# Which way pairs 14 and 15 are turned: TensorE, or DRAM and transposing DMAs

## The chip, the cores and the metric

The kernel runs on one core of a Trainium2 chip. The metric is the device time of one execution in microseconds (us). The core has a matrix engine (TensorE, in profiles PE, its weight loads PEld), three engines for elementwise work (VectorE or DVE, ScalarE or ACT, GpSimd or POOL), and SyncE (SP), whose queue issues most of this kernel's transfers. The core's 16 DMA engines move the data between DRAM and the on-chip memory (SBUF). Matmuls write their results into the 8 banks of a second memory, PSUM.

## The reference

Causal attention with 16 extra "beacon" keys in front, followed by a feed-forward net of three maxed branches:

```python
B, H, S, D, Nb = 8, 8, 576, 64, 16
k_all = concatenate([beacon_k, k], axis=2)        # beacons are seen by every query
v_all = concatenate([beacon_v, v], axis=2)
scores = matmul(q, k_all.T) / sqrt(D)             # later keys masked out
a = exp(scores - max) ; a /= a.sum(-1)
attn = matmul(a, v_all)                           # (B, H, S, D)
x = attn.transpose(0, 2, 1, 3).reshape(B * S, H * D)       # 4608 x 512
h = maximum(maximum(x @ w1, x @ w2), x @ w3)      # 512 -> 768
out = h @ w_out                                   # 768 -> 512
```

Inputs and output are float32.

## The kernel before

The 64 heads (8 batches of 8) are worked off as 32 **pairs** of heads, four pairs to a batch; pair p belongs to batch p // 4. Two pairs make a quad. One pass of the main loop is a **step** and belongs to one pair.

To multiply q and k, TensorE needs them with the head's 64 dimensions on the partitions, that is, transposed. Four buffers `qTs` and four `kTs` hold transposed pairs, pair p in buffer p % 4. There are two ways in which a pair gets there, and both start alike: `load_pair` (L225) brings q and k as float32 into a staging tile `st` (a rotation of 8 tiles, which V's pieces share), and `cast_pair` (L260, on GpSimd) makes bfloat16 tiles of them (rotations of 4 each).

- **On TensorE**, pairs 0 to 15: `turn_pair(p)` makes 12 transposes of 96 x 128 (six for q, six for k, L387) into two PSUM banks. VectorE copies k out of PSUM (L433), ScalarE or VectorE copies q (L422), and `place_beacons` (L429) copies the 16 beacon columns of k from `bT`, where they lie ready.
- **Through DRAM**, pairs 16 to 31: `store_pair` (L372) writes the bfloat16 tiles to a scratch tile in DRAM, and `fetch_pair` (L379 and L380) reads them back with DMAs that transpose. `open_dram` (L363) makes the scratch tiles of a batch and writes its beacons ahead of k, so that they come along with the fetch.

In the main loop, from pair 8 on, a step p emits this:

1. `emit_burst(p)`: 12 score matmuls (L495) into all 8 PSUM banks, with ScalarE's exponentials (L513) behind them into `at_sb`.
2. At even p, `emit_pv_whole`: the 72 matmuls of values and sums (L615) of the two pairs before.
3. GpSimd's causal masks (L535) on this pair's `at_sb`.
4. Units of the feed-forward net (L691 for the first layer, L739 for the second), as many as a schedule allows. Output tiles y go out on SP's queue (L771). After the first unit stands `turn_pair(p + 1)`, if pair p + 1 is turned on TensorE; after the second unit, the work that `plan` holds for (p, 0). What it holds for (p, 1) comes at the end of the step.

`plan` is filled by hand, by step. For a pair p turned on TensorE the cast stands in step p - 2. For a pair through DRAM the cast stands in step p - 5, the store in step p - 4 and the fetch in step p - 3. Each cast is followed by `next_load`, which issues the next load of the list `loads`; that list is sorted by the step in which the loaded data is cast, and within a step by a second number (0 for pairs turned on TensorE, 1 for pieces of V, 2 for pairs through DRAM). With the load of pair 16 go the loads of the beacon keys of batches 4 to 7, which are cast together in step 11 (`bk16`). Those of batches 1 to 3 were cast long before (`bk16_1`).

All loads, stores, fetches and outputs stand in SP's one queue, in the order in which they are emitted. An instruction that waits there holds all that are behind it.

Of the kernel before, what the change touches and what calls it, by code (L numbers as in the profile page):

```python
# [17 lines left out]
def kernel(  # L18
# [15 lines left out]
    B, H, S, D = q.shape  # L34
    Nb = beacon_k.shape[2]
# [25 lines left out]
    PPB = H // 2  # L61
    PPQ = PPB // n_quad
    NPAIR = B * PPB
    RING = 4

    B_PE = 4

# [46 lines left out]
    ffn_h = ctx.enter_context(tc.tile_pool(name="ffn_h", bufs=2))  # L116
    ffn_y = ctx.enter_context(tc.tile_pool(name="ffn_y", bufs=5))
    psum = ctx.enter_context(tc.tile_pool(name="psum", bufs=1, space=PSUM))
    dram_pool = ctx.enter_context(tc.tile_pool(name="dram", bufs=B - B_PE, space=bass.MemoryType.DRAM))

    N_BANK = 8
    acc = psum.tile([128, N_BANK, 512], FP32, name="acc")
# [48 lines left out]
    xT = const.tile([128, n_ct, RING * S], BF16, name="xT")  # L171
    NB_PE = Nb * B_PE
    NB_DMA = Nb * (B - B_PE)
    bT = const.tile([128, PPB, NB_PE], BF16, name="bT")
# [3 lines left out]
    bk16_1 = const.tile([NB_PE - Nb, H, D], BF16, name="bk16_1")  # L178
    bk32 = const.tile([NB_DMA, H, D], FP32, name="bk32")
    bk16 = const.tile([NB_DMA, H, D], BF16, name="bk16")  # L180
# [153 lines left out]
    def load_beacons(b0, b1, dst, queue=None):  # L334
        for b in range(b0, b1):
            (queue or nc.sync).dma_start(
                out=dst[Nb * (b - b0) : Nb * (b - b0 + 1)],
                in_=beacon_k[b].rearrange("h n d -> n h d"),
            )
# [19 lines left out]
    def open_dram(b):  # L359
        q_dram[b] = dram_pool.tile([PPB, S, 2 * D], BF16, name="q_dram")  # L360
        k_dram[b] = dram_pool.tile([PPB, NK, 2 * D], BF16, name="k_dram")
        lo = Nb * (b - B_PE)
        nc.sync.dma_start(  # L363
            out=k_dram[b][:, 0:Nb].rearrange("i n x -> n i x"),
            in_=bk16[lo : lo + Nb].rearrange("n (i h) d -> n i (h d)", h=2),
        )

    def store_pair(p):
# [135 lines left out]
    def emit_burst(p):  # L504
        at[p] = at_pool.tile([128, AT_W], BF16, name="at_sb")
        for gi, first in enumerate(next_pairs()):
            off = 0
            for t, q0, q1 in groups(p)[gi]:
                for e in range(2):
                    score(p, t, e, q0, q1, acc[:, first + e, off : off + q1 - q0])  # L510
                off += q1 - q0
            for e0, e1 in ((0, 1), (1, 2)) if gi == 0 else ((0, 2),):
                nc.scalar.activation(  # L513
                    out=both_heads(p, gi)[:, e0:e1],
                    in_=acc[:, first + e0 : first + e1, 0 : g_width(p, gi)],
                    func=AF.Exp,
                    scale=scale,
                )
# [250 lines left out]
    def store_y(n):  # L769
        for c0, y in y_out[:n]:  # L770
            nc.sync.dma_start(out[c0 : c0 + 128, :], y)  # L771
        del y_out[:n]
# [20 lines left out]
    def may_emit(limit, ahead=0):  # L793
        n = done[0] + ahead
        return n < END and n + 1 <= limit + 1e-6 and units[n][0] <= ready[0]
# [13 lines left out]
    def at_step(p, g, *fns):  # L809
        plan.setdefault((p, g), []).extend(fns)  # L810

    def L(fn, *a):
        return lambda: fn(*a)

    def cast_step(p):
        return (p - 2, 0) if p < B_PE * PPB else (p - 5, int(p < 19))

    def v_step(b, piece):
        return (b * PPB + 1, piece)

    def load_turned_pair(p, **gate):
        if p == B_PE * PPB:
            load_beacons(B_PE, B, bk32)
        load_pair(p, **gate)

    loads = [(cast_step(p), 2 * (p >= B_PE * PPB), partial(load_turned_pair, p)) for p in range(2 * PPB, NPAIR)]
    loads += [(v_step(b, i), 1, partial(load_v, b, i)) for b in range(2, B) for i in range(2)]
    loads = [load for _, _, load in sorted(loads, key=lambda x: x[:2])]

# [5 lines left out]
    def C(fn, *a):  # L835
        def run():
            fn(*a)
            next_load()

        return run  # L840

    def start():
        keep_busy(8, 480)
        load_half(0, 0, nc.sync)
        load_half(0, 1, nc.scalar)
        load_half(1, 0, nc.sync)
        load_beacons(0, 1, bk32_0, nc.scalar)
        load_half(1, 1, nc.scalar)
        make_identity(nc, ident)
        nc.gpsimd.memset(tri, 1.0)  # L850
        nc.gpsimd.affine_select(
            out=tri,
            in_=tri,
            compare_op=ALU.is_ge,
            fill=0.0,
            base=0,
            pattern=[[1, 128]],
            channel_multiplier=-1,
        )
        load_quad(1, 0)  # L860
        load_quad(0, 1)
        load_quad(1, 1)
        load_v(0, 0)
        load_v(0, 1)
        load_beacons(1, B_PE, bk32_1)
        cast_half(0, 0, by_dve)
        cast_half(0, 1, by_act)
        by_dve(bk16_0, bk32_0)
        turn_part(0, 0, 0, 6, by_act)
        turn_part(0, 0, 1, 7)  # L870
        keep_busy(3)
        turn_beacons(0, 1, bk16_0)
        cast_half(1, 0, by_dve)
        cast_half(1, 1, by_dve)
        keep_busy(2)
        turn_part(1, 0, 0, 4)
        turn_part(1, 0, 1, 5)
# [94 lines left out]
    def second_batch():  # L972
        for p in range(PPB, 2 * PPB):
            place_beacons(p + 1, by_act)
            emit_burst(p)
            for gi in range(NG):
                emit_masks(p, gi)
                if p < PPB + 2 and 0 < gi < 3:
                    cast_piece(p + 2, gi - 1, by_pool)
                if p == 2 * PPB - 1 and gi == 1:  # L980
                    cast_v(1, 1, by_pool)
                    next_load(gate=nc.gpsimd)
                    next_load(3)
            if p < PPB + 2:
                stage.pop(("pair", p + 2))
            if p == PPB + 2:
                load_w_out()
                cast_v(1, 0, by_pool)
            if p + 1 < 2 * PPB:
                turn_pair(p + 1, by_dve)  # L990
                F(2, next_psum)
        F(4, next_psum)
        for p in range(2 * PPB, 2 * PPB + 2):
            cast_pair(p, by_pool, by_pool)
            next_load()
        finish = emit_pv_whole(n_quad)
        turn_pair(2 * PPB, by_dve)
        F(2, next_psum)
        finish()

    for p in range(B_PE * PPB, NPAIR):
        if p % PPB == 0:
            at_step(p - 4, 0, L(open_dram, p // PPB))
        at_step(p - 3, 0, L(fetch_pair, p))
        at_step(p - 4, 0, L(store_pair, p))
    for p in range(2 * PPB + 2, B_PE * PPB):
        at_step(*cast_step(p), C(cast_pair, p, by_pool, by_pool))
    for b in range(2, B):
        for i in range(2):
            at_step(*v_step(b, i), C(cast_v, b, i, by_pool))  # L1010
    at_step(B_PE * PPB - 5, 1, L(by_pool, bk16, bk32))
    for p in range(B_PE * PPB, NPAIR):
        at_step(*cast_step(p), C(cast_pair, p, by_pool, by_pool))


    def emit_all():
        start()
        first_batch()
        second_batch()
        n_y = 0  # L1020
        v_tiles.pop(0)

        for p in range(2 * PPB, NPAIR):
            b, pi = divmod(p, PPB)
            emit_burst(p)
            finish = emit_pv_whole(p // 2 - 1) if p % 2 == 0 else None
            for gi in range(NG):
                emit_masks(p, gi)
            allowed = (b - 1) * UPB + (-2, 4, 10, 16)[pi]
            n = 0  # L1030
            while may_emit(allowed):
                n_y = len(y_out)
                close = not may_emit(allowed, 1)
                emit_ffn(allowed, last_pair() if close else next_psum, close)
                store_y(n_y)
                n += 1
                if n == 1 and p + 1 < B_PE * PPB:
                    turn_pair(p + 1, by_act)
                    place_beacons(p + 1, by_act)
                if n == 2:  # L1040
                    for fn in plan.pop((p, 0), ()):
                        fn()
            assert n >= 2
            if finish:
                finish()
            for s in range(2):
                for fn in plan.pop((p, s), ()):
                    fn()
            if pi == 0:
                v_tiles.pop(b - 1)  # L1050
        assert not plan and not loads
        finish = emit_pv_whole(NPAIR // 2 - 1)
        for _ in range(4):
            emit_ffn(END, next_psum)
        finish()
        store_y(len(y_out))
        while emit_ffn(END - 1, next_psum):
            store_y(len(y_out))
        mm2_last(n_tokb - 1, TOKB // 128 - 1, (0, 320, 512))
# [33 lines left out]
```

## Time and profile before

| | |
|---|---|
| median of 3 runs | 286.55 us (285.75 to 287.72) |
| the profiled execution | 285.18 us, span 283.5 us |
| granted TensorE clock | 1.00 |
| TensorE | 97% busy; 144 transposes at L387 |
| VectorE, ScalarE, GpSimd | 61%, 56%, 48% busy |
| stores `q_dram<-p`, `k_dram<-p` | 16 each, 144 KB, median 2.3 us to landing |
| fetches `qT<-q_dram`, `kT<-k_dram` | 16 each, median 4.3 and 3.5 us to landing |
| loads of q and k per pair | 28 each, 288 KB, median 5.3 and 5.5 us to landing |

The span runs from the first to the last instruction of the profiled execution; 1.7 us of its time lie around it. The profile is of a single execution, 1.37 us below the median of the timed runs. "To landing" counts from the start of the issuing instruction on its queue to the moment when the data is there, and so has in it the time that a transfer stands behind others.

### The profile page before, as it was taken

To read this page: it belongs to the slowest core of one execution; us is meant where nothing else is said; L and a number is where in the kernel's file an instruction comes from. 1 tells how busy PE (TensorE), PEld (TensorE's weight loads), DVE (VectorE), ACT (ScalarE), POOL (GpSimd) and SP (SyncE) were. 2 spreads that over 40 slices of the span, in tenths; PEclk is the share of its full clock that TensorE was granted. 3 is DMA by queue.
4 is the path that set the end of the run, shared out by engine and by line. 5 is a ranking of instruction groups with operands and counts; after the bars stand their busy time and mean duration, and the time that the engine had idled before them with its cause. 6 is when DMAs were issued, how large, how long until landed. Compare 5 with 4: busy or idle time off the path is not lost.

```text
span 283.5 us, 7622 instructions
## 1 busy us (share of the span) xinstructions
PE 274.7 (97%) x2996; PEld 156.4 (55%) x2996; DVE 172.7 (61%) x303; ACT 159.4 (56%) x299; POOL 136.4 (48%) x282
## 2 busy tenths in 40 slices
PE   7889999999999999999999999999999999999995
PEld 3466664555555555555556787555555554444442
DVE  3774765583856658274836383638363847876873
ACT  3697595896668576858585858585767640000000
POOL 7263789287376865466556746583346210000000
PEclk9999999999999999999999999999999999999999
DMA  7999999999999999999999999999451003004004
GB/s 146 193 198 222 246 225 178 240 201 295 276 226 235 255 265 203 226 222 240 250 213 225 267 254 183 216 258 218 121 156 39 0 2 146 2 1 150 0 0 148
DMA packets 85315, 50.59 MB, mean 178 GB/s; under 512 B 64416, under 2 KB 80032, under 8 KB 85280
## 3 DMA queue, kind: packets, MB, share of 16 engines
q1 hardware_dynamic: 80672, 45.76, 71.8%
q0 software_dynamic: 4048, 4.03, 9.0%
q8 instruction: 23, 0.38, 0.6%
q10 hardware_dynamic: 560, 0.33, 0.5%
q14 instruction: 12, 0.10, 0.1%
HBM read 35.13 MB, written 14.22 MB: 174 GB/s over the span
## 4 chain that ended last, share of the span: by engine, by line
PE 82%; DVE 1%; issue 0%
PE acc L691 46%; PE acc L739 16%; PE acc L615 11%; PE acc L495 7%; PE acc L387 2%; PE acc L757 0%; DVE hT L709 0%; DVE qT L422 0%; DVE y L764 0%; DVE kT L433 0%
## 5 line engine op out<-in xcount | busy, mean ns | idle before, releaser
L691 PE MATMUL acc<-xT,w_sb 128*128 128x512 bf16 (+4 forms) x744 | 135.3, 338 | 0.0
L709 DVE TENSOR_TENSOR hT<-hT,acc 128x512 bf16<-128x512 bf16 x102 | 70.0, 687 | 59.2 <-PE acc L691 50.0
L691 PEld LDWEIGHTS <-w_sb 128*128 128x128 bf16 x744 | 69.2, 98 | 59.7
L535 POOL TENSOR_SCALAR_AFFINE_SELECT at_sb<-at_sb 128x256 bf16<-128x256 bf16 (+2 forms) x176 | 62.8, 378 | 71.1 <-ACT at_sb L513 69.4
L513 ACT ACTIVATE at_sb<-acc 128x208 bf16<-128x208 f32 (+3 forms) x140 | 89.5, 737 | 5.9 <-PE acc L495 4.6
L260 POOL CAST p<-st 96x768 bf16<-96x768 f32 x56 | 44.7, 821 | 9.3 <-PE acc L615 5.1
L739 PE MATMUL acc<-w_out_sb,hT 128*128 128x512 bf16 (+2 forms) x246 | 48.4, 348 | 0.0
L711 ACT CAST hT<-acc 128x352 bf16<-128x352 f32 x18 | 8.1, 452 | 47.0 <-PE acc L691 47.0
L739 PEld LDWEIGHTS <-hT 128*128 128x128 bf16 x246 | 22.6, 98 | 21.7 <-DVE hT L709 1.6
L746 DVE COPY y<-acc 128x512 f32<-128x512 f32 (+1 forms) x35 | 21.9, 628 | 20.5 <-PE acc L739 14.8
L711 DVE CAST hT<-acc 128x512 bf16<-128x512 f32 (+1 forms) x48 | 26.6, 554 | 9.4 <-PE acc L691 9.1
L495 PE MATMUL acc<-qT,kT 64*128 64x208 bf16 (+1 forms) x336 | 26.9, 280 | 1.1 <-DVE hT L730 0.6
L764 ACT COPY y<-acc 128x320 f32<-128x320 f32 x1 | 0.4, 426 | 46.0 <-PE acc L757 46.0
L495 PEld LDWEIGHTS <-kT 64*128 64x128 bf16 x336 | 15.5, 94 | 13.3 <-issue 2.6
L615 PE MATMUL acc<-at_sb,v_sb 128*32 128x512 bf16 (+5 forms) x672 | 22.8, 281 | 0.0
L638 DVE TENSOR_TENSOR xT<-raw,recip 128x576 bf16<-128x576 f32 x28 | 21.8, 821 | 0.0
L625 ACT COPY raw<-acc 128x512 f32<-128x512 f32 x28 | 15.8, 637 | 4.5 <-PE acc L615 4.3
L305 POOL CAST v_sb<-st 128x1536 bf16<-128x1536 f32 (+2 forms) x21 | 18.3, 893 | 0.0
L615 PEld LDWEIGHTS <-v_sb 128*32 128x32 bf16 (+1 forms) x672 | 14.5, 96 | 6.7
L489 ACT ACTIVATE at_sb<-acc 128x1024 bf16<-128x1024 f32 (+3 forms) x16 | 13.1, 860 | 3.6 <-PE acc L480 3.5
L615 PE MATMUL acc<-at_sb,ones 128*32 128x512 bf16 (+3 forms) x336 | 14.9, 284 | 0.0
L433 DVE COPY kT<-acc 128x576 bf16<-128x576 bf16 x12 | 9.0, 752 | 6.3 <-PE acc L387 6.3
(69 smaller groups left out, 170.5 us busy)
## 6 DMA issues: line engine op xcount, KB each, us to landing
out_dram<-y SPq DMA_DIRECT2D x35, 256.0 KB, 3.5
st<-in_q_dram SPq DMA_DIRECT2D x28, 288.0 KB, 5.3
st<-in_k_dram SPq DMA_DIRECT2D x28, 288.0 KB, 5.5
st<-in_v_dram SPq DMA_DIRECT2D x24, 256.0 KB, 6.7
w_sb<-in_moe_w_dram POOLq DMA_DIRECT2D x6, 384.0 KB, 7.7
q_dram<-p SPq DMA_DIRECT2D x16, 144.0 KB, 2.3
k_dram<-p SPq DMA_DIRECT2D x16, 144.0 KB, 2.3
st<-in_v_dram SPq DMA_DIRECT2D x8, 224.0 KB, 6.4
```

Source lines behind the costliest of these rows:

```text
L260: cast(t16.rearrange("p r h d -> p h r d"), st[0:QP, i * NQ2 : (i + 1) * NQ2].rearrange("p (h r d) -> p h r d", h=2, r=QR),)
L305: cast(v_sb[0:n, t:t1].rearrange("p t h d -> p (t h d)"), st[0:n, (t - t_lo) * H * D : (t1 - t_lo) * H * D],)
L495: nc.tensor.matmul(ps, kTs[p % NT][hs, 128 * t : 128 * t + 128], qTs[p % NT][hs, q0:q1], start=True, stop=True, tile_position=(64 * e, 0),)
L513: nc.scalar.activation(out=both_heads(p, gi)[:, e0:e1], in_=acc[:, first + e0 : first + e1, 0 : g_width(p, gi)], func=AF.Exp, scale=scale,)
L535: nc.gpsimd.affine_select(out=view, in_=view, compare_op=ALU.is_ge, fill=0.0, base=x0, pattern=[[0, 2], [1, hi - lo]], channel_multiplier=-1,)
L615: nc.tensor.matmul(acc[32 * j : 32 * j + 32, bank, lo + q0 - qa : lo + qb - qa], lhsT, at_view(PPQ * quad + j // 2, t, j % 2, q0, qb), sta ...
L638: nc.vector.tensor_mul(xT[:, 2 * g + i, c0 : c0 + S], raw[:, i], recip)
L691: nc.tensor.matmul(ps[:, a:b], w_in[i][:, ct, 128 * ft : 128 * (ft + 1)], xT[:, ct, x0 : x0 + b - a], start=(ct == 0), stop=(ct == n_ct - 1),)
L709: nc.vector.tensor_max(h[:, lo:hi], h[:, lo:hi], ps[:, lo:hi])
L711: (by_act if hi < TOKB else by_dve)(h[:, lo:hi], ps[:, lo:hi])
L739: nc.tensor.matmul(ps[:, lo:hi], hT[:, ft, 128 * tt : 128 * (tt + 1)], w_out_sb[:, ft, lo:hi], start=(ft == 0), stop=(ft == n_ft - 1),)
L746: (by_act if hi < d_model else by_dve)(y[:, lo:hi], ps[:, lo:hi])
```

## The change

A number `FIRST_DMA = 14` takes the place of `B_PE * PPB = 16` where the kernel decides which pairs go through DRAM. Pairs 14 and 15, the last two of batch 3, are cast in steps 10 and 11 (instead of 12 and 13), stored in steps 11 and 12 and fetched in steps 12 and 13, all three one step later against their burst than for pairs 16 and up. Batch 3 gets scratch tiles in DRAM, of which these two pairs use the second half; its beacons are written there, for all four pairs, from `bk16_1`. The loads of pairs 14 and 15 get the second number 2, and their place in the list of loads follows the new cast steps. `turn_pair` and `place_beacons` are no longer called for these two.

```diff
+    FIRST_DMA = 14
...
-    dram_pool = ctx.enter_context(tc.tile_pool(name="dram", bufs=B - B_PE, space=bass.MemoryType.DRAM))
+    dram_pool = ctx.enter_context(tc.tile_pool(name="dram", bufs=B - FIRST_DMA // PPB, space=bass.MemoryType.DRAM))
...
     def open_dram(b):
...
-        lo = Nb * (b - B_PE)
+        src, lo = (bk16, Nb * (b - B_PE)) if b >= B_PE else (bk16_1, Nb * (b - 1))
...
-            in_=bk16[lo : lo + Nb].rearrange("n (i h) d -> n i (h d)", h=2),
+            in_=src[lo : lo + Nb].rearrange("n (i h) d -> n i (h d)", h=2),
...
     def cast_step(p):
-        return (p - 2, 0) if p < B_PE * PPB else (p - 5, int(p < 19))
+        if p < FIRST_DMA:
+            return (p - 2, 0)
+        return (p - 4, 0) if p < B_PE * PPB else (p - 5, int(p < 19))
+
+    def store_step(p):
+        return p - 3 if p < B_PE * PPB else p - 4
...
-    loads = [(cast_step(p), 2 * (p >= B_PE * PPB), partial(load_turned_pair, p)) for p in range(2 * PPB, NPAIR)]
+    loads = [(cast_step(p), 2 * (p >= FIRST_DMA), partial(load_turned_pair, p)) for p in range(2 * PPB, NPAIR)]
...
-    for p in range(B_PE * PPB, NPAIR):
-        if p % PPB == 0:
-            at_step(p - 4, 0, L(open_dram, p // PPB))
-        at_step(p - 3, 0, L(fetch_pair, p))
-        at_step(p - 4, 0, L(store_pair, p))
-    for p in range(2 * PPB + 2, B_PE * PPB):
+    for p in range(FIRST_DMA, NPAIR):
+        if p == FIRST_DMA or p % PPB == 0:
+            at_step(store_step(p), 0, L(open_dram, p // PPB))
+        at_step(store_step(p) + 1, 0, L(fetch_pair, p))
+        at_step(store_step(p), 0, L(store_pair, p))
+    for p in range(2 * PPB + 2, FIRST_DMA):
         at_step(*cast_step(p), C(cast_pair, p, by_pool, by_pool))
...
-    for p in range(B_PE * PPB, NPAIR):
+    for p in range(FIRST_DMA, NPAIR):
         at_step(*cast_step(p), C(cast_pair, p, by_pool, by_pool))
...
-                if n == 1 and p + 1 < B_PE * PPB:
+                if n == 1 and p + 1 < FIRST_DMA:
                     turn_pair(p + 1, by_act)
                     place_beacons(p + 1, by_act)
```

## The prediction

> **What bounds the kernel now.** I read the page's first two parts, then the chain of waits in order of time, then SP's timeline, and last single transfers (issue and landing). The page first: the engines' busy time, and the busy tenths in 40 slices.
>
> ```profile
> PE 274.7 (97%) x2996; PEld 156.4 (55%) x2996; DVE 172.7 (61%) x303; ACT 159.4 (56%) x299; POOL 136.4 (48%) x282
> ...
> PE   7889999999999999999999999999999999999995
> ...
> DMA  7999999999999999999999999999451003004004
> ```
>
> TensorE is full from the fourth slice on, at a granted clock of 1.00. But the DMA engines are full too, up to about 200 us, and the change takes work from the first and gives it to the second. So two things are to be read: how much of TensorE's time the removed transposes are, and how far ahead of TensorE the transfers run. The chain that ended last, stage by stage (start, length, engine and line):
>
> ```profile
> 90.34 0.84 PE acc L495 x12
> 91.18 1.40 PE acc L739 x6
> 92.58 0.51 PE acc L387 x12
> 93.09 1.30 PE acc L739 x6
> 94.39 3.46 PE acc L691 x20
> 97.85 0.85 PE acc L495 x10
> 98.70 2.25 PE acc L615 x71
> 100.95 0.97 PE acc L691 x4
> 101.92 0.51 PE acc L387 x12
> 102.43 4.33 PE acc L691 x24
> 106.76 0.85 PE acc L495 x11
> ...
> 120.45 0.83 PE acc L495 x12
> 121.28 2.70 PE acc L739 x12
> 123.98 3.46 PE acc L691 x20
> 127.44 0.85 PE acc L495 x11
> 128.29 2.25 PE acc L615 x72
> 130.54 5.29 PE acc L691 x28
> ```
>
> L495 opens the step of each pair: 13 at 90.34, 14 at 97.85, 15 at 106.76, 17 at 120.45, 18 at 127.44, 19 at 135.84 (the next line of that view). From 53 us to the end every piece is TensorE's and each starts where the last ends, so no other engine and no transfer holds it up, and what is taken out of it there comes off the end. L387 is the turning: pair 14 at 92.58 in step 13, pair 15 at 101.92 in step 14.
>
> **What is removed.** 24 transposes, 12 for each pair. In the chain 12 cost 0.51 us, 43 ns each. A second way gives the same: step 17 has the matmuls of step 13 without a turn, and step 18 those of step 14. 7.51 - 6.99 = 0.52 and 8.91 - 8.40 = 0.51. So **1.03 us leave the path**. The same comparison says what happens without the two PSUM banks of a turn: steps 17 and 18 run so and show no gap, so I add nothing for banks. Two copies on VectorE (L433, mean 752 ns) and four on ScalarE (L422, 648, and L429, 228) go as well, 1.5 and 1.75 us; neither engine is on the path (61% and 56% busy), so this gains nothing. The groups' table gives a transpose a mean of 206 ns, which would make 24 of them 4.9 us; but 12 start within 0.51 us, so they overlap, and the chain's 43 ns is the price.
>
> [...]
>
> **What is added, on the queue of SP.** Four transposing transfers (L379, L380, issue 1.14 and 1.23 us), four stores (L372, 0.38 to 0.52), one of beacons (L363, 0.57 to 1.30): about 4.8 + 1.8 + 0.9 = 7.5 us, in steps 11 to 13. SP's own waits say what can cover this: between 75.6 and 113 us it stood 1.2 + 0.8 + 2.4 + 1.2 + 1.5 + 0.8 = 7.9 us for other engines. SP's order there now:
>
> ```profile
> 77.56 7.98 SPq L289 DMA_DIRECT2D st<-in_v_dram  x5
> 85.66 1.30 SPq L363 DMA_DIRECT2D k_dram<-bk  x1
> ...
> 93.85 1.24 SPq L379 DMA_TRANSPOSE qT<-q_dram  x1
> 95.15 1.24 SPq L380 DMA_TRANSPOSE kT<-k_dram  x1
> ```
>
> The third of the five V pieces is issued at 79.05 and holds the queue for 4.09 us: here SP goes as fast as transfers land. The first fetch now is pair 16's, issued at 93.85 and landed 3.3 and 2.6 us after each issue, at 97.7, for a burst that starts at 112.9: 15 us early. Pair 14 has less: its fetch stands one step later against its burst (two steps ahead, not three), and its burst starts at 97.85 - 0.52 = **97.3**.
>
> When does it land? Transfers of the queue land one behind the other. Up to that V piece the same loads go out as now, in another order, so it still lands at 79.05 + 8.1 = 87.1. Behind it come, by the gaps between landings now: beacons 0.2; store of pair 14 0.5 (87.05 + 2.3 and 87.52 + 2.2) to 1.2 (the slow store at 109.44); two V pieces 1.9 (landed 88.4 and 89.0); loads of pairs 18 and 19, four at 1.0 (landings 75.5, 76.6, 77.5, 78.4); the two transposing transfers at 0.4 to 0.6. That is 87.1 + 0.2 + 0.8 + 1.9 + 4.0 + 1.0 = **95.0, 2.3 us in time**. SP itself is at the fetch by about 89.5 and done at 92, so the queue of transfers decides. Fastest rows (0.5 for the store, 0.4 per transpose) give 94.5. With the slowest (1.2 for the store, 1.6 per load as at 87.94, 0.6 per transpose) it is 98.0, a stall of 0.7 us, less than is saved. I take 95.0: most loads of that stretch are near 1.0.
>
> Next comes pair 15, fetched in step 13 ahead of pair 16. Behind 95.0 stand two stores, beacons, the load of pair 20 and three output tiles: some 2.0 + 0.2 + 3.5 + 1.6, then its own 1.0, so 103.3 against a burst at 106.76 - 1.03 = 105.7: 2.4 us in time. Pair 17's k landed at 113.4; the added transfers, some 4 us of the queue's time (two pairs of 0.8 + 1.0, and 0.2), all still ahead of it, make 117.4 against 119.4. From step 15 on SP waits for TensorE again (2.0 us at most, to reuse qT), so the delay ends there.
>
> **What is moved on GpSimd.** The casts stay 56 in number (0.82 us each). Pair 14's go to step 10, 72.7 to 74.3, ahead of masks that start at 76.56; its load moves ahead to where pair 13's is now (landed at 71.2, 1.5 us ahead of the cast). Pair 13's load slips by some 3.5 us, to about 74.7, for a cast at 80.05; pair 15's lands near 76.7 for one at 81.6; 16 and 17 keep 4 us. Pair 15's casts lengthen step 11 by 1.6 us, so burst 12's masks end near 88.4 instead of 86.8; step 14 reads them from 98 on. Pair 17's cast now needs the buffer that pair 14's store frees at 87.9 to 88.5, up to 1 us later than GpSimd could start; behind it are burst 13's masks, due at 91.3. All of this is hidden, by 3 us or more; with that cover gone, the late thing would be the mask, and step 14's sums of values with it.
>
> **The sum.** The profiled execution took 285.18 us (span 283.5, 1.7 around it), 1.37 under the median of the runs. 285.18 - 1.03 = 284.15; on the median, 286.55 - 1.03 = **285.5 us**. One per cent is 2.9 us, about what a measurement tells from no change here (the runs span 0.7%), so the forecast is "within 1%, on the fast side".
>
> **The rivals.**
>
> A: *the fetch of pair 14 is late, and TensorE waits at step 14.* If SP reaches it no earlier than it reaches its first fetch now (93.85) and it lands as slowly as pair 17's q did (6.1 us, k 0.4 behind), k is there at 100.4: a stall of 3.1, net +2.1, **288.6**. For it: full DMA slices, and 8 us from issue to burst, where pair 17's fetch has 13.6 (106.9 to 120.45). Against: nothing ahead of it in the queue waits for an output tile any more. From a landing at 98.3 on it makes the change a loss, from 101.2 on one of over 1%. [...]
>
> B: *none of SP's 7.5 us is absorbed*, and pair 17's fetch lands at 113.4 + 7.5 = 120.9 against 119.4: 1.5 lost, 1.0 saved, **287.0**. Against: the 7.9 us of waits.
>
> C: *the saved microsecond turns into a wait* for a PSUM bank or a mask in steps 13 and 14: **286.5**. Against: steps 17 and 18.
>
> D: *more is saved*, the transposes being worth their 206 ns: 286.55 - 4.9 = **281.6**. Against: back-to-back pieces in the chain.
>
> **Chances.** Forecast 0.66, A 0.15 (0.07 of it over 1%, where pair 15 is late too), B 0.06 (0.01 over 1%), C 0.08, D 0.05. Faster by over 1% is D and the forecast's luckiest edge, 0.06; slower 0.08; the rest, 0.86, is within 1%. The range starts at 283.9 (the lowest run, 285.75, less 1.03, less 0.8 for its own spread) and ends at 288.6, A's time; C and B lie inside.
>
> **What would show it.** No L387 in steps 13 and 14; step 13 about 6.99 us and step 14 about 8.40; 120 transposes at L387 instead of 144; L379 and L380 18 times each, the first issued near 89.5. Pair 14's k landing near 95, pair 15's near 103. DMA's full slices reach a little further, and TensorE's chain stays without gaps. Wrong would be: a score at L495 in steps 14, 15 or 17 that waits for a transfer, or steps 13 and 14 that are not shorter.

## The result, and the profile after

The change makes the kernel **slower: ratio 1.0074, 95% interval 1.0051 to 1.0097** (medians 288.65 us against 286.15, 22 runs each). The ratio is that of the mean times, without three executions of the changed kernel (290.7 to 292.3 us) that count as slow. Forecast was 285.5, 1.03 us faster. The profiled execution took 288.68 us, its span is 287.0 where it was 283.5; this 3.5 us is more than the 2.1 us of the ratio, because the profiled execution of before lies 1.0 us under its median. From here on a line number of the changed kernel is one higher than in the kernel before (scores L496, fetches L380 and L381).

The page of the changed kernel, engines' busy time and busy tenths in 40 slices:

```profile
PE 275.6 (96%) x2972; PEld 155.6 (54%) x2972; DVE 170.7 (59%) x301; ACT 158.4 (55%) x295; POOL 136.6 (48%) x282
...
PEclk9999999999999999999997999999999999999999
DMA  7999999999997999999999999989945003003004
```

24 matmuls fewer (x2972 for x2996), yet TensorE's busy time has grown by 0.9 us, and the granted clock has a 7 in one slice. The chain that ended last says where (start, length, what), first around pair 15, then around pair 21:

```profile
91.01 0.84 PE acc L496 x12
...
98.01 0.85 PE acc L496 x11
98.86 1.51 PE acc L616 x40
100.36 0.29 SPq L380
...
100.70 5.77 DMA kT<-k_dram
106.47 0.05 issue
106.52 0.88 PE acc L496 x12
```

```profile
141.78 0.85 PE acc L496 x11
142.62 2.25 PE acc L616 x71
144.88 0.98 PE acc L692 x4
145.86 0.33 SPq L380
...
146.23 4.90 DMA kT<-k_dram
151.14 0.05 issue
151.18 0.88 PE acc L496 x12
152.06 4.38 PE acc L740 x12
```

The turning is gone, and steps 13 and 14 are as short as forecast: 7.00 us (91.01 to 98.01) and 8.51 to burst 15, of which 0.11 is a first short wait. But the chain now leaves TensorE for a transfer twice. Burst 21, seven steps behind the last changed one, starts at 151.18 where 7.54 us after burst 20 (141.78) was due: it waits **1.86 us** for k of its own pair. Behind it 12 matmuls of L740 take 4.38 us; the same 12 take 2.70 in step 17 of the kernel before. Busy times in stretches (us, engines, then PEclk, DMA share, GB/s) show why:

```profile
152.00:156.40 4.40, 4.40 (x18) 1.71 (x15) 0.69 (x1) 2.73 (x4) 2.68 (x7) 0.61 0.93 187
156.40:160.00 3.60, 3.60 (x41) 3.17 (x40) 2.76 (x4) 0.29 (x1) 3.39 (x5) 1.00 1.07 240
```

A clock of 0.61 over 4.40 us costs another **1.7 us**. The span adds up: burst 13 starts 0.67 later than in the execution of before (no step ahead of it that the change touches is longer), -1.0 for the turns, +0.1, +1.9 and +1.7, together 3.4 of the 3.5.

SP's queue, kernel before and changed kernel, at the fetch of pair 21:

```profile
137.70 1.16 SPq L379 DMA_TRANSPOSE qT<-q_dram  x1
138.90 1.26 SPq L380 DMA_TRANSPOSE kT<-k_dram  x1
```

```profile
145.06 1.13 SPq L380 DMA_TRANSPOSE qT<-q_dram  x1
146.23 1.58 SPq L381 DMA_TRANSPOSE kT<-k_dram  x1
```

k landed 4.0 us after its issue in the kernel before, at 142.9 for a burst at 149.5: a lead of 6.6 us. In the changed kernel it is issued 7.3 us later and lands 4.9 behind that. So what the added transfers cost the queue in steps 11 to 13 was still missing seven steps later.

SP's queue around the fetch of pair 18, again in both kernels, shows what SP waits for in these steps:

```profile
109.44 0.52 SPq L372 DMA_DIRECT2D q_dram<-p  x1
...
111.33 1.15 SPq L289 DMA_DIRECT2D st<-in_v_dram  x2
113.85 1.13 SPq L379 DMA_TRANSPOSE qT<-q_dram  x1
```

```profile
117.32 0.52 SPq L373 DMA_DIRECT2D q_dram<-p  x1
...
118.36 1.16 SPq L290 DMA_DIRECT2D st<-in_v_dram  x2
119.94 1.27 SPq L380 DMA_TRANSPOSE qT<-q_dram  x1
```

In the kernel before, the store issued at 109.44 landed 4.3 us later, at 113.77, and the fetch of the same pair went out 0.08 us behind that, after 1.4 us of waiting. In the changed kernel the store landed at 119.89, and the fetch went out 0.05 us later. In both kernels the fetches of pairs 19, 22 and 23 too go out 0.05 to 0.08 us behind the landing of their own store. The buffer was not what they waited for: burst 14, the last to read the one that pair 18 gets, had ended at 98.70 in the kernel before.

### The profile page after: what moved, and what is told of

It is laid out like the page before. It is cut to its first block, busy times and chain, and to the rows that moved or that the text cites. A ratio compares the mean times of both kernels' runs of the same rounds, so it can differ in the third digit from the quotient of the medians.

```text
span 287.0 us, 7580 instructions
## 1 busy us (share of the span) xinstructions
PE 275.6 (96%) x2972; PEld 155.6 (54%) x2972; DVE 170.7 (59%) x301; ACT 158.4 (55%) x295; POOL 136.6 (48%) x282
## 4 chain that ended last, share of the span: by engine, by line
PE 78%; DMA 4%; DVE 1%; issue 0%; SPq 0%
PE acc L692 43%; PE acc L740 16%; PE acc L616 11%; PE acc L496 7%; DMA kT<-k_dram 4%; PE acc L388 1%; PE acc L758 0%; DVE hT L710 0%; DVE qT L423 0%; SPq L380 0%; DVE y L765 0%; DVE kT L434 0%
## 5 line engine op out<-in xcount | busy, mean ns | idle before, releaser
L740 PE MATMUL acc<-w_out_sb,hT 128*128 128x512 bf16 (+2 forms) x246 | 50.0, 356 | 0.0
L740 PEld LDWEIGHTS <-hT 128*128 128x128 bf16 x246 | 23.0, 99 | 23.3 <-issue 2.3
L496 PE MATMUL acc<-qT,kT 64*128 64x208 bf16 (+1 forms) x336 | 26.8, 280 | 4.3 <-DMA kT<-k_dram 1.9
L496 PEld LDWEIGHTS <-kT 64*128 64x128 bf16 x336 | 15.4, 94 | 16.7 <-issue 3.6
L639 DVE TENSOR_TENSOR xT<-raw,recip 128x576 bf16<-128x576 f32 x28 | 20.7, 781 | 0.0
L721 PE MATMUL acc<-xT,w_sb 128*128 128x256 bf16 x96 | 12.0, 273 | 0.3 <-DMA w_sb<-in_moe_w_dram 0.3
```

The lines of the kernel that those rows point to most:

```text
L496: nc.tensor.matmul(ps, kTs[p % NT][hs, 128 * t : 128 * t + 128], qTs[p % NT][hs, q0:q1], start=True, stop=True, tile_position=(64 * e, 0),)
L639: nc.vector.tensor_mul(xT[:, 2 * g + i, c0 : c0 + S], raw[:, i], recip)
L740: nc.tensor.matmul(ps[:, lo:hi], hT[:, ft, 128 * tt : 128 * (tt + 1)], w_out_sb[:, ft, lo:hi], start=(ft == 0), stop=(ft == n_ft - 1),)
```

## The experiments

Ratios are to the kernel before, run on the same chip; intervals are of 95%. Two theories were set against each other from e4 on: **S**, what is full is SP's one queue, instruction by instruction; **D**, what is full are the 16 DMA engines, byte by byte.

| run | what | ratio |
|---|---|---|
| e1_turns_out | turns of 14 and 15 out, no transfers | 0.9967 (0.9942 to 0.9991) |
| e2_transfers_added | transfers in, turns kept | 1.0128 (1.0094 to 1.0163) |
| e3_one_pair | change for pair 15 alone | 1.0030 (1.0002 to 1.0057) |
| e4_stores_act | changed, stores on ScalarE's queue | 1.0194 (1.0165 to 1.0222) |
| e5_stores_pool | changed, stores on GpSimd's queue | 1.0046 (1.0026 to 1.0066) |
| e6_tiny | before, 16 loads of 4 KB added | 1.0115 (1.0086 to 1.0143) |
| e7_big | before, 3 stores of 786 KB added | 1.0034 (1.0009 to 1.0058) |
| e8_stores_added | as e2, without the transposing four | 1.0017 (1.0000 to 1.0034) |
| e9_pool_later | as e5, stores behind V's casts | 0.9994 (0.9959 to 1.0028) |
| e10_merged | changed, q and k in one transfer | 0.9982 (0.9950 to 1.0014) |
| e11_merged_before | before, q and k in one transfer | 1.0015 (0.9988 to 1.0043) |
| e12_merged_12 | as e10, from pair 12 on | 1.0141 (1.0103 to 1.0179) |
| e13_merged_pool | e9 and e10 together | **0.9962 (0.9939 to 0.9985)** |
| e14_short_fetches | as e2, fetches of 16 rows | 1.0066 (1.0032 to 1.0100) |

### The two terms apart: e1 and e2

```diff
# e1, in the kernel before
-                if n == 1 and p + 1 < B_PE * PPB:
+                if n == 1 and p + 1 < 14:
```

> Pairs 14 and 15 are not turned on TensorE and nothing takes the place of the turn (their scores are made of what the buffers held, pairs 10 and 11); no transfer is added. This takes the first term of the sum by itself. If the price of the turn was right, steps 13 and 14 last 7.0 and 8.4 us and the time is 1.03 us under the kernel before, ratio 0.9964, about 285.1. If the turn was hidden behind something, steps 13 and 14 stay at 7.5 and 8.9 and the time at 286.2.

Ratio 0.9967, where 0.9964 was worked out. Its chain has burst 13 at 90.10 and burst 14 at 97.09, a step of 6.99 us. The turn is worth what the forecast said.

```diff
# e2, in the kernel before; the spare places lie over the dead bk32_0 and bk32_1
+    at_step(11, 0, open_extra)
+    for n in range(2):
+        at_step(12 + n, 0, L(fetch_extra, n))
+        at_step(11 + n, 0, L(store_extra, n))
```

> The kernel before, with the added transfers alone: the bfloat16 tiles of pairs 12 and 13 are stored and fetched as well, in the steps and the order of the change (beacons and a store in step 11, fetch and store in 12, fetch in 13), into spare buffers that nobody reads. All 16 pairs are still turned on TensorE and no load or cast moves. Theory T, the transfers alone cost the lead: the fetches of pairs 17 to 25 land 6 to 8 us later than in the kernel before, one or more bursts wait, TensorE's clock is halved behind a wait of some 2 us, and the time is 287.5 to 290. Rival O, the new order of loads and casts costs it: fetches land as before and the time is 286.2.

Ratio 1.0128, with no load or cast moved and every turn kept. So the transfers alone make a loss as large as the change's, and the rival, the new order, isn't needed for it. 0.9967 x 1.0128 = 1.0095, at the upper end of the change's interval. The profiled execution has the waits at pairs 21 and 25 (chain of waits, each line k's landing):

```profile
144.06 5.43 DMA kT<-k_dram
...
175.40 5.23 DMA kT<-k_dram
```

### Half the change: e3

```diff
-    FIRST_DMA = 14
+    FIRST_DMA = 15
```

> The change for pair 15 alone (FIRST_DMA = 15). If the loss of lead goes with the number of transfers, the fetches behind lose 3 to 4 us of their lead, the smallest lead of before (5.2 us at pair 25) is not used up, no burst waits and half the turning time is gained: 0.5 us under before, 285.7. If the queue has no lead to give (the lead of one profiled execution being no measure of the other runs), the time is between the two kernels, about 287.3.

1.0030, between the two expectations and above 1: half the turns are gained (0.0017) and something near 0.0047 is paid. That speaks for a loss without a threshold: the lead of one profiled execution isn't a reserve that all executions have. Of the 19 executions of the changed kernel that the ratio counts, 9 have a mean clock of 0.994 or less; of the 23 of the kernel before that were run beside this one, 5. Where those 5 lost their clock isn't known: in e5's profiled execution (mean clock 0.994) the one slice under 0.9, a 7, lies at 7 to 14 us, ahead of every fetch. So that the kernel before has executions with such waits too, and that every lost microsecond of lead makes more of them, is likely, but not shown.

### What in the transfers costs: e6, e7, e8, e14

```diff
# e6, in the kernel before
+    def tiny(n):
+        lo = 16 * (n % 8)
+        nc.sync.dma_start(out=(big_0, big_1)[n // 8][lo : lo + 16, 0:D], in_=q[0, 0, lo : lo + 16])
+    for n in range(16):
+        at_step(11 + n // 6, 0, L(tiny, n))
# e7, in the kernel before
+    for n in range(3):
+        at_step(11 + n, 0, L(store_copy, n))   # w_in[n] to a DRAM tile, 786 KB
# e8: e2 without the line of fetch_extra
# e14: e2 with in_=extra[...][2 + n, 0:16]
```

> The kernel before with 16 added loads of 4 KB on SP's queue in steps 11 to 13, into a spare place: some 16 x 0.45 = 7.2 us of SP's time, as much as the change adds, and 0.06 MB. Theory S: the fetches of pairs 17 to 25 lose 5 to 8 us of lead, ratio 1.008 to 1.015, as with the added transfers of the pairs. Theory D: nothing is lost, ratio 0.998 to 1.002.

> The kernel before with three added stores of 786 KB on SP's queue, one in each of steps 11, 12 and 13 (a weight tile written to a place that nobody reads): 2.4 MB, twice what the change writes and reads, in three instructions of 0.5 us. Theory D: the DMA engines have no room, the fetches of pairs 17 to 25 lose 8 us or more, ratio 1.01 or more. Theory S: each delays what is behind it by some 3 us, SP makes it up, and from pair 19 on the lead is that of the kernel before; ratio 0.998 to 1.004.

> The kernel before with the added beacons and stores alone (of the added transfers, the four that transpose are left out): 4 x 0.45 + 0.9 = 2.7 us of SP's time and 0.6 MB of writing. If the price goes by SP's time, a third of the loss of lead, 2.5 us, no burst waits at 21 and 25 in most runs, ratio 1.001 to 1.005, and the transposing transfers are the dear part of the 1.0128. If it goes by bytes, half of it, ratio about 1.006.

> The kernel before with the added transfers of pairs 12 and 13, where each of the four transposing transfers fetches 16 rows instead of 576 or 592; stores and beacons whole. With the whole fetches the ratio was 1.0128, with none 1.0017. If a transposing transfer costs the queue by the instruction, 1.008 to 1.013; if by its rows, 1.001 to 1.005.

0.06 MB in 16 instructions cost 1.0115, about as much as the pairs' transfers; 2.4 MB in three cost 1.0034. Theory D alone can't have that: it gave e6 nothing and e7 1.01 or more. e6's page shows what happens (mean busy share of the DMA engines, and GB/s, by slices):

```profile
DMA  7999999999967999999999999999944003003004
GB/s 149 195 192 222 225 225 193 244 199 299 278 141 135 296 186 252 221 190 255 226 229 223 171 255 260 199 205 265 214 106 167 2 2 120 26 1 149 0 0 147
```

In the twelfth and thirteenth slices, 79 to 93 us, the engines run at 141 and 135 GB/s instead of 226 and 235: they have room while SP hands them small things. The changed kernel's line has a 7 of its own in the thirteenth. SP's queue in e6, six of the small loads:

```profile
87.57 3.98 SPq L1005 DMA_DIRECT2D bk<-in_q_dram  x6
```

0.66 us for each, and 11.8 us for all 16, more than the 0.45 and 7.2 assumed. In e6's profiled execution one burst waited, 1.3 us at pair 25; another 1.9 us of its longer span lie ahead of the edit, in a start-up that differs by up to 2.6 us between the profiled executions.

But theory S was not right in full either. It had e7's fetches back on time by pair 19. In e7's profiled execution the lead (from k's landing to the burst) at pairs 19 and 21 was 8.9 and 1.3 us, where the kernel before has 11.7 and 6.6 and e6 8.0 and 0.8, and pair 25's k was late by 0.4 us. So three big stores took nearly as much lead as 16 small loads, and bytes count too. And e8's 2.7 us in the queue (1.0017) cost next to nothing: its leads at pairs 17, 21 and 25 are 6.9, 6.6 and 5.1 us, those of the kernel before 7.0, 6.6 and 5.2, so that much is absorbed. The dear part of the change is the four transposing transfers, 1.0128 less 1.0017. With 16 rows each in place of 576 or 592 about half of that is left (1.0066), so they cost **both by the instruction and by their rows**. The four took 1.10 to 1.22 us each on SP with 16 rows, and 1.30 to 2.30 with all their rows. How an instruction's price divides into its time on SP and its place among the transfers in flight, no run here settles.

### Relieving the queue: e4, e5, e9, e10, e11, e12, e13

```diff
# e4 and e5, in store_pair of the changed kernel
-            nc.sync.dma_start(
+            nc.scalar.dma_start(      # e4;   nc.gpsimd.dma_start( in e5 and e9
# e9: in steps 13, 17, 21 and 25 the store stands at (step, 1), behind cast_v
# e10, e11, e12: one tile qkT for q and k, one scratch tile, one store, and
+        nc.sync.dma_start_transpose(out=qks[p % NT][:, 0 : S + NK], in_=rows[0 : S + NK])
```

> The changed kernel, with the stores of the pairs (q_dram and k_dram, 36 of 144 KB) issued on ScalarE's queue instead of SP's: the same bytes, 0.9 us less for SP in every step from 11 on. Theory S, SP's issuing in order is what is full: the lead comes back, no burst waits, and the time is about 1 us under the kernel before, 285.1 to 285.6. Theory D, the 16 DMA engines are what is full: the bytes are the same, the fetches are as late as in the changed kernel and the time is 288 to 289.

1.0194, and not what either theory said: ScalarE itself stood still at its stores. Its longest such wait, in the view of waits (total, times, longest):

```profile
ACT hT L712 <- DMA q_dram<-p: 4.0, 1, 4.0
```

The casts, copies and exponentials behind it were late, and TensorE waited for banks that ScalarE had not read (5.5 us at L496). The run says nothing on S against D.

> The changed kernel with the stores of the pairs issued on GpSimd's queue instead of SP's: GpSimd has made the tiles, so it waits for nothing, and its masks have some 3 us to spare; ScalarE is not touched, which in the run with the stores on ScalarE's queue stood up to 4 us behind its own stores. Theory S, SP's one queue is what is full (issue time, and few transfers in flight): fetches land with the lead of the kernel before or more, no burst waits, ratio 0.995 to 1.000. Theory D, the 16 DMA engines are full: same bytes, fetches as late as in the changed kernel, ratio 1.005 to 1.010. If GpSimd is held by its own transfers, masks are late and step 14 and the like wait for them.

1.0046, between the two expectations; its interval overlaps the change's. The lead was back (3.4 and 4.1 us at pairs 21 and 25) and no burst waited for a fetch; instead (view of waits)

```profile
PEld L616 <- POOL v_sb L306: 2.1, 6, 0.5
```

the values' matmuls of steps 18, 22 and 26 waited half a microsecond each for V's casts, which stood behind two stores of 0.51 us on GpSimd.

> The changed kernel with the stores on GpSimd's queue, and in steps 13, 17, 21 and 25 behind the casts of V: in the run with the stores on GpSimd's queue the fetches had their lead back (3.4 and 4.1 us at pairs 21 and 25), but steps 18, 22 and 26 lasted 8.89 us instead of 8.40, waiting for V's casts behind the stores. If that is all that stood between that run and the gain of the turn, steps 18, 22 and 26 are back at 8.40 and the ratio is 0.996 to 0.999. If GpSimd's part of the transfers costs something else, it stays at 1.002 to 1.005.

Steps 18, 22 and 26 are back at 8.40, 8.46 and 8.40 us, as in the kernel before. The ratio, 0.9994, lies just outside what was expected for that, and its interval reaches from a gain to a loss.

> The changed kernel, with q and k of a pair in one scratch tile and in one SBUF tile, so that each pair through DRAM is one store and one transposing transfer (1168 rows) instead of two of each; bytes as in the changed kernel. If SP pays by the instruction, it saves some 1.2 + 0.45 us in every step from 12 on, far more than the change adds, the lead grows from step to step, no burst waits, and the ratio is 0.996 to 0.998. If a transposing transfer costs SP by its rows (2.3 us for the one), only 0.45 us a step is saved, the lead at pairs 21 and 25 is 1 to 4 us, ratio 0.998 to 1.003. If the DMA engines are what counts, it is the changed kernel again, 1.0074.

> The same merging in the kernel before (pairs 16 to 31 only). TensorE was never waiting there in the profiled execution, so a longer lead can gain nothing but the waits of disturbed executions: ratio 0.998 to 1.000. The lead of its fetches against the kernel before (7.0, 6.6 and 5.2 us at pairs 17, 21 and 25) shows what merging gives back: by the instruction, 8 us or more at pair 21.

e10 came to 0.9982, with 1 in its interval, and no burst waited in its profiled execution. But the lead did not grow from step to step as paying by the instruction had it (3.7, 4.6 and 4.5 us at pairs 17, 21 and 25). One transposing instruction of 1168 rows goes out in 1.22 us at best, little more than one of 576, and yet in e11 k of pairs 21 and 25 lands only 1.5 and some 3 us earlier against its burst than in the kernel before. In e11 SP stood 6.4 us between 113 and 150 waiting for stores to land before it could issue their fetches: the same wait as shown above for pair 18.

> As the merged changed kernel, with pairs 12 and 13 through DRAM too (FIRST_DMA = 12): two more turns of 0.51 us off TensorE, 0.9928 to 0.995 if merging leaves enough of SP's queue; over 1.0 if the fetch of pair 12, in step 10 where loads of many pairs and of V stand ahead of it, lands after burst 12 has to start at 82.

1.0141: the second outcome, but for more than the reason expected. TensorE's waits from 64 to 90 us (view of waits):

```profile
PE acc L616 <- POOL v_sb L310: 2.0, 2, 1.2
PE acc L496 <- DMA qkT<-qk_dram: 1.4, 1, 1.4
```

Pair 12's fetch goes out at 82.5, and burst 12 waits 1.4 us for it, until 87.2 instead of 82. Most of these 5 us came earlier: in step 10 the values' matmuls waited 2.0 us for casts of V, whose pieces landed late. The mean clock of this execution was 0.994 over its span of 286.8 us, another 1.7 us; with the 2.0 and the 1.4 that makes up the 5, if it was lost ahead of burst 12.

> The changed kernel with both remedies: one store and one transposing transfer a pair, the store on GpSimd's queue (behind V's casts where both are in a step). Each alone came to 0.9994 and 0.9982. If the lead is what was short, the fetches keep 6 us or more at pairs 21 and 25, no burst waits in any but disturbed executions, and the ratio is that of the turn alone, 0.995 to 0.998. If the remedies do not add, 0.998 to 1.001.

**0.9962 (0.9939 to 0.9985)**, faster than the kernel before, and so than the changed one, and e1's 0.9967 in full. The lead did not come out as expected: 2.6 and 6.3 us at pairs 21 and 25, and 0.8 at pair 14. No burst of the profiled execution waited for a fetch even so, and all 12 executions have a mean clock of 0.998 or more. Steps 13 and 14 in stretches:

```profile
90.90:97.89 6.99, 6.99 (x45) 3.50 (x45) 5.32 (x8) 3.50 (x7) 4.84 (x10) 1.00 1.17 297
97.89:106.29 8.40, 8.40 (x115) 4.66 (x114) 3.67 (x6) 6.10 (x13) 6.30 (x13) 1.00 1.13 316
```

Full clock, no wait, and 297 and 316 GB/s where the changed kernel moved 256 and 244: with SP relieved the engines move more in these steps.

## Why the prediction was wrong

- **What bounds the kernel, and the gain of 1.03 us: right.** Shown by e1 (0.9967) and by steps 13 and 14. The chain's 43 ns was the price, not the 206 ns of the table.
- **The landing of pair 14: 95.0 forecast, 97.6 measured**, 0.4 us ahead of its burst instead of 2.3. The V piece at the head of the sum landed at 86.8 as worked out (87.1); the rest was mis-sized: beacons and store took 2.2 us where the sum had 1.0, and the two V pieces and four loads 7.6 (from k's store at 89.0 to 96.6) where it had 5.9. The two transposing transfers took the 1.0 of the sum.
- **Pair 15: 103.3 forecast against 105.7; measured 106.5**, and burst 15 waited 0.1 us for it. Of the 3.2 us, 2.6 came over from pair 14's landing.
- **"From step 15 on SP waits for TensorE again (2.0 us at most, to reuse qT), so the delay ends there": this step failed.** The view of waits names TensorE there, but the buffer that pair 18's fetch writes had been free for 15 us (98.70 to 113.85), and the fetch went out 0.08 us behind the landing of its own pair's store. Such a wait wasn't free time: the late queue issued the store at 117.32 instead of 109.44, the store landed at 119.89 instead of 113.77, and the wait moved along. At 137.70 the fetch of pair 21 had been 6.6 us ahead; it came 7.3 us later, so nothing had been given back. The sum looked at pairs 14, 15 and 17 and stopped, where in the kernel before the leads at pairs 21 and 25 (6.6 and 5.2 us) were smaller than at 17 (7.0).
- **Rival B was the mechanism, with the wrong price.** It had the 7.5 us unabsorbed, but let only pair 17 pay (1.5 us). Pair 17's k landed at 119.6, forecast 120.9, 0.6 us in time; pair 21 paid, and in e2 pair 25 as well. The 7.9 us of waits between 75.6 and 113 us were the argument against it, and in the changed kernel they covered next to nothing: pair 17's fetch was issued 7.9 us later, 0.7 of them from the later start. That e8's 2.7 us were absorbed says that SP had some slack, but less than these waits suggested.
- **A wait was priced at its length.** At pair 21 1.86 us of waiting cost 3.6, because of the clock (0.61 over the next 4.40 us). No rival had that term.
- **Rival C: not seen**, as steps 13 and 14 were as short as forecast. **Rival A** had the place nearly right, as pairs 14 and 15 came within 0.4 us, but not the size: it had pair 14's k at 100.4 and a stall of 3.1 us, where that k landed at 97.6 (pair 14's and 15's k landed 0.5 and 1.4 us behind their q). For this kernel as it stands TensorE is the better place for the turning of these pairs (1.0074 through DRAM); with the queue relieved, in e13, it is not (0.9962).

## What to carry to other kernels

SP's queue serves a full engine here, and had a lead (5.2 us at its smallest, at pair 25) but little slack (the fetch of pair 21 came 7.3 us later): in such a queue look for the smallest lead over the whole rest of the program, and take an added transfer from that, not from the step in which it is issued. Before a wait of the queue is counted as slack, find out what ends it: here the waits for the queue's own stores gave nothing back of those 7.3 us. Count instructions in the issuing queue as well as bytes; here 16 loads of 4 KB cost more than three stores of 786 KB. When work is moved to a loaded queue, move something off it in the same change: with the stores on GpSimd's queue and one transposing transfer where there were two, the same idea went from 1.0074 to 0.9962.

## What the runs showed of the hardware

In the changed kernel's trace a wait of 1.87 us on TensorE, up to 151.18, was followed by 3.41 us at a granted clock of 0.50 (152.15 to 155.56; 0.61 as the mean over the 4.40 us from 152.00), which cost about as much as the wait. It doesn't always follow: in e2 a wait of 1.8 us ahead of burst 25 left the clock at 1.00 (178.30 to 187.70), and in e4, where the longest wait at L496 was 1.9 us, every slice of the granted clock shows a 9. What sets these cases apart, no run here shows.
